# A linear-attention and two-layer MoE kernel: the broadcast of inverse roots to the rows of a head issued per head instead of per pair of heads

## Chip, cores and metric

The kernel runs on one core of one Trainium2 chip. The metric is device time in microseconds (us) of one execution. Three executions of the kernel before took 1691.96, 1692.08 and 1693.05 us; their median, 1692.08 us, is the time before.

## What is computed

The reference is a linear attention over 8 batches, 8 heads, 576 positions and a head size of 64, with a root-mean-square normalization of each position of each head, and then two pairs of dense layers on the 4608 tokens (batch times position) of width 512, each with an inner width of 2048:

```python
kv = einsum('bhsd,bhse->bhde', k, v)
out = einsum('bhsd,bhde->bhse', q, kv)
rms = sqrt(mean(out * out, axis=-1) + 1e-06)
x = (out / rms * g_norm)              # to (4608, 512)
h = x @ w1_in;  x = (s * relu(h)**2 + b) @ w1_out
h = x @ w2_in;  out = (h * sigmoid(1.702 * h)) @ w2_out
```

The part that matters here is `out / rms`: one number, the inverse root, belongs to each of the 8 heads and each token, and must multiply the 64 rows of that head.

## The kernel before

Tokens lie along the free dimension. They are cut into nine blocks j of 512 tokens. A block's attention output is four tiles of 128 rows (two heads of 64 rows each) by 512 tokens, one per pair p. All matmuls of the dense layers are done in a high and a low part (three products in place of one), and most blocks go through a seven-product scheme (`PRODUCTS`) in place of eight plain products.

`events` is a list written by hand: each step has a slot number, the list is sorted by slot, and every engine and queue gets its instructions in that one order. Nearly all transfers are issued from one queue, that of SyncE (SP), in that order. A transfer on SP takes one of eight completion semaphores in turn (DMAHW0 to DMAHW7 in the order listings below), and waits until the transfer eight places before it, which had the same one, has landed.

For the blocks j = 1 to 8, `attend` (line 745) places the attention. The steps that the prediction speaks of, by line:

- `att_product` (L342) and `att_square` (L351) make the output and its squares; `block_mean` (L396) adds the squares of each head on TensorE, so that the result has one row for 16 partitions per head; `block_root` and `block_newton` (L363 to L370) make the inverse roots.
- `y_store` (L411) writes the eight rows of inverse roots, 8 x 512 floats or 16 KB, to a buffer in HBM, `yd[j]`.
- `y_load` (L416) reads them back for each pair p: two rows of 2 KB each, each written to 64 partitions of the tile `yb`, 256 KB in all. It must wait until the store has landed. There are 4 such loads a block, 32 in the program.
- `att_scale` (L421, VectorE) multiplies the attention output by `yb`; `att_split` then splits the result in high and low part (L438, L441) for the first blocks, or stores it (L428) in HBM for the blocks from 3 on.

Behind a block's four `y_load` there stand on SP, by part of the program: loads of raw weights (L133, L138) for the conversion of the first layer's weights, loads of q (L293) and of k and v (L275, L278, L280) for later blocks, stores of converted weights (L190, L203, L243), and in the seven-product part the loads of weights `wl` (L254), each of which feeds two products of TensorE (L565). In the plain part TensorE's steps are `mlp_h` (L479) and `mlp_o` (L522).

Of the kernel before, what the change touches and what calls it, by code (L numbers as in the profile page):

```python
# [14 lines left out]
T = 512  # L15
B, H, S, D = 8, 8, 576, 64
# [47 lines left out]
def kernel(ctx: ExitStack, tc: tile.TileContext, q_h, kv_h, kt, vt, cst,  # L64
# [6 lines left out]
    nc = tc.nc  # L71
# [22 lines left out]
    def new2(dtype, name):  # L94
        return new(mid, [P, T], dtype, name)
# [174 lines left out]
    yd = [dp.tile([H, T], F32, name=f"yd{j}") for j in range(NB)]  # L270
# [142 lines left out]

    def y_load(j, p):
        y = new2(F32, "yb")
        nc.sync.dma_start(out=y, in_=yd[j][2 * p:2 * p + 2].unsqueeze(1).to_broadcast([2, D, T]))  # L416
        att[j, p] = (att[j, p][0], y)

    def att_scale(j, p):
# [325 lines left out]
    def attend(j, slot, gap, late):  # L745
        for g in range(NG):
            at(slot - 4 + g, q_load, j, g)
            at(slot + gap * g, att_product, j, (2 * g, 2 * g + 1))
            for r in range(2):
                at(slot + gap * g + 0.4 + 0.3 * r, att_square, j, 2 * g + r)  # L750
                at(slot + gap * g + 0.4 + 0.3 * r, att_copy, j, 2 * g + r)
        slot += gap + 1.4
        at(slot, block_mean, j)
        at(slot + 0.5, block_root, j)
        at(slot + 1.2, block_newton, j)
        at(slot + 1.8, y_store, j)
        for p in range(NP):
            at(slot + 2.7, y_load, j, p)
            at(slot + late + 1.1 * p, att_scale, j, p)
            at(slot + late + 1.1 * p + 0.3, att_split, j, p)  # L760
# [263 lines left out]
```

## Time and profile before

| | |
|---|---|
| Median of three executions | 1692.08 us |
| Profiled execution, its own time | 1698.42 us |
| Span of the profile | 1696.6 us |
| Mean granted clock of TensorE | 0.956 |
| TensorE matmul busy | 1553.9 us, 92% of the span |
| VectorE, ScalarE busy | 63% and 47% |
| DMA moved | 392.09 MB, mean 231 GB/s |

The span runs from the first to the last instruction; the execution's own time is 1.8 us longer. The profiled execution is 6.3 us longer than the median. Busy shares are averages over the whole span: the first 750 us hold the attention, the conversion of the weights and the plain part, the rest is nearly all matmul. "SPq" is the SP queue issuing a transfer; the time of such a row is that of the issue, not of the transfer.

### The profile page before, as it was taken

To read this page: it belongs to the slowest core of one execution; us is meant where nothing else is said; L and a number is where in the kernel's file an instruction comes from. 1 tells how busy PE (TensorE), PEld (TensorE's weight loads), DVE (VectorE), ACT (ScalarE), POOL (GpSimd) and SP (SyncE) were. 2 spreads that over 40 slices of the span, in tenths; PEclk is the share of its full clock that TensorE was granted. 3 is DMA by queue.
4 is the path that set the end of the run, shared out by engine and by line. 5 is a ranking of instruction groups with operands and counts; after the bars stand their busy time and mean duration, and the time that the engine had idled before them with its cause. 6 is when DMAs were issued, how large, how long until landed. Compare 5 with 4: busy or idle time off the path is not lost.

```text
span 1696.6 us, 20384 instructions
## 1 busy us (share of the span) xinstructions
PE 1553.9 (92%) x7316; PEld 1251.2 (74%) x7316; DVE 1065.3 (63%) x1535; ACT 794.0 (47%) x1162; POOL 1.5 (0%) x12
## 2 busy tenths in 40 slices
PE   7978995969966997879999999999999999999999
PEld 4656764758654875658888888888888888888887
DVE  5966352535654855549467437977896888579522
ACT  5967441425545834558259522542443245135222
POOL 0000000000000000000000000000000000000000
PEclk8999996979987999879999999999999999999999
DMA  9435337496677875698698257678578757837590
GB/s 313 146 108 184 128 139 257 150 315 226 225 256 252 309 231 209 226 327 279 209 387 285 99 217 263 231 273 305 189 266 306 276 198 274 291 106 246 195 328 25
DMA packets 176484, 392.09 MB, mean 231 GB/s; under 512 B 21952, under 2 KB 53696, under 8 KB 176384
## 3 DMA queue, kind: packets, MB, share of 16 engines
q1 hardware_dynamic: 176384, 390.79, 65.9%
q8 instruction: 58, 0.95, 0.2%
q14 instruction: 42, 0.34, 0.1%
HBM read 300.42 MB, written 90.31 MB: 230 GB/s over the span
## 4 chain that ended last, share of the span: by engine, by line
PE 76%; DMA 13%; DVE 6%; SPq 3%; ACT 1%; issue 1%; DVEq 0%; ACTq 0%
PE o L522 22%; PE o L693 18%; PE a L565 8%; PE d L565 8%; PE h L479 6%; PE b L565 4%; PE c L565 4%; PE f L565 4%; DMA wl<-wsd 3%; DMA raw<-in_w_in 1%; DMA wsd<-op 1%; DMA qq<-in_q 1%; DVE cu L157 1%; DMA yb<-yd 1%; DMA raw<-in_w_out 1%; SPq L416 1%
## 5 line engine op out<-in xcount | busy, mean ns | idle before, releaser
L522 PE MATMUL o<-gh,w 128*128 128x512 f32 x1280 | 408.3, 392 | 1.0 <-DVE w L173 0.8
L522 PEld LDWEIGHTS o<-gh,w 128*128 128x128 f32 x1280 | 241.0, 189 | 57.7 <-issue 3.5
L693 PE MATMUL o<-gh,wl 128*128 128x512 f32 x896 | 276.4, 389 | 0.0
L522 PE MATMUL o<-gl,w 128*128 128x512 f32 x640 | 250.2, 391 | 0.3 <-DVE gl L512 0.2
L565 PE MATMUL a<-xh,wl 128*128 128x512 f32 x448 | 160.7, 400 | 45.8 <-DMA wl<-wsd 45.8
L693 PEld LDWEIGHTS o<-gh,wl 128*128 128x128 f32 x896 | 168.2, 188 | 34.9
L479 PE MATMUL h<-xh,w 128*128 128x512 f32 x512 | 173.9, 401 | 17.8 <-ACT w L168 9.9
L565 PE MATMUL d<-xh,wl 128*128 128x512 f32 x448 | 157.9, 393 | 19.9 <-DMA wl<-wsd 16.1
L693 PE MATMUL o<-gl,wl 128*128 128x512 f32 x448 | 174.3, 389 | 0.0
L522 PEld LDWEIGHTS o<-gl,w 128*128 128x128 f32 x640 | 120.7, 189 | 25.8 <-DVE gl L512 1.2
L565 PEld LDWEIGHTS a<-xh,wl 128*128 128x128 f32 x448 | 86.2, 192 | 67.8 <-issue 34.4
L479 PEld LDWEIGHTS h<-xh,w 128*128 128x128 f32 x512 | 97.7, 192 | 47.4 <-ACT w L168 10.3
L581 ACT ACTIVATE c<-a 128x512 f32<-128x512 f32 x56 | 33.4, 597 | 194.9 <-PE a L565 192.0
L565 PEld LDWEIGHTS d<-xh,wl 128*128 128x128 f32 x448 | 84.6, 189 | 40.4 <-issue 16.4
L479 PE MATMUL h<-xl,w 128*128 128x512 f32 x256 | 101.6, 397 | 0.4 <-DVE xl L441 0.4
L693 PEld LDWEIGHTS o<-gl,wl 128*128 128x128 f32 x448 | 84.1, 188 | 17.5
L636 DVE TENSOR_TENSOR gl<-r,gh 128x512 fp32r<-128x512 f32 x96 | 65.2, 687 | 40.2 <-PE o L522 23.2
L565 PE MATMUL a<-xl,wl 128*128 128x512 f32 x224 | 89.1, 398 | 0.0
L584 DVE TENSOR_TENSOR u<-b,c 128x512 f32<-128x512 f32 x56 | 38.6, 690 | 79.4 <-PE b L565 49.7
L565 PE MATMUL d<-xl,wl 128*128 128x512 f32 x224 | 87.7, 391 | 0.0
L667 ACT ACTIVATE gh<-t 128x1024 fp32r<-128x1024 f32 x48 | 51.0, 1062 | 72.5 <-DVE t L658 62.4
L620 ACT ACTIVATE r<-r 128x1024 f32<-128x1024 f32 x84 | 84.5, 1052 | 0.0
(114 smaller groups left out, 2539.6 us busy)
## 6 DMA issues: line engine op xcount, KB each, us to landing
wl<-wsd SPq DMA_DIRECT2D x168, 512.0 KB
wl<-wo2S SPq DMA_DIRECT2D x64, 512.0 KB
wsd<-op SPq DMA_DIRECT2D x96, 256.0 KB
w<-wod SPq DMA_DIRECT2D x48, 512.0 KB
wl<-wo2A SPq DMA_DIRECT2D x48, 512.0 KB
raw<-in_w_in SPq DMA_DIRECT2D x32, 512.0 KB
raw<-in_w_out SPq DMA_DIRECT2D x32, 512.0 KB
wl<-wsd SPq DMA_DIRECT2D x56, 256.0 KB
```

Of the source, the lines that this page charges most:

```text
L157: dve.scalar_tensor_tensor(out=t, in0=raw[:, :, 1], scalar=SIGN_TOP, in1=t, op0=ALU.bitwise_and, op1=ALU.bitwise_or)
L416: nc.sync.dma_start(out=y, in_=yd[j][2 * p:2 * p + 2].unsqueeze(1).to_broadcast([2, D, T]))
L479: pe.matmul(h, lhsT=a, rhs=b, start=(n == 0), stop=(n == 3 * NP - 1))
L522: pe.matmul(acc[m, j][c], lhsT=a, rhs=x, start=(f == 0 and n == 0), stop=(f == NF - 1 and n == 2))
L565: pe.matmul(o, lhsT=a, rhs=b, start=(first and n == 0), stop=(n == 5), skip_group_check=not first)
L581: act.activation(st["c1"], st[0], AF.Copy)
L584: dve.tensor_add(out=st["u2"], in0=st[1], in1=st["c1"])
L620: act.activation(R[q, n], R[q, n], fn)
L636: dve.tensor_sub(out=gl, in0=R[q, i][:, half, :], in1=gh.bitcast(F32))
L667: act.activation(hi, src, AF.Copy)
L693: pe.matmul(so[k, d], lhsT=a, rhs=b, start=(first and n == 0 and i == 0 and e == 0), stop=(n == 3 and i == 1 and e == 2), skip_group_check ...
```

## The change

The load of one pair's two rows, [2 heads, 64 copies, 512], becomes two loads, one per head, [64 copies, 512]. The bytes are the same, 256 KB a pair. There are now 64 loads of 128 KB on SP instead of 32 of 256 KB, at the same places in the order.

```diff
     def y_load(j, p):
         y = new2(F32, "yb")
-        nc.sync.dma_start(out=y, in_=yd[j][2 * p:2 * p + 2].unsqueeze(1).to_broadcast([2, D, T]))
+        for h in range(2):
+            nc.sync.dma_start(out=y[h * D:(h + 1) * D], in_=yd[j][2 * p + h:2 * p + h + 1].to_broadcast([D, T]))
         att[j, p] = (att[j, p][0], y)
```

On the SP queue at block 1, in the plain part, this stands before (`yd` is the buffer of inverse roots, `raw` a tile of raw weights; a name with _49 is a semaphore):

```order
L133 DMA raw<-in_w_in 128x4x256 [waits DMAHW0_49,Activation_49]
L416 DMA yb<-yd_139 128x1x512 [waits DMAHW7_49,DMAHW1_49,PE_49]
L416 DMA yb<-yd_139 128x1x512 [waits DMAHW2_49,PE_49]
L416 DMA yb<-yd_139 128x1x512 [waits DMAHW3_49,Activation_49]
L416 DMA yb<-yd_139 128x1x512 [waits DMAHW4_49]
L138 DMA raw<-in_w_out 128x1024 [waits DMAHW5_49]
L133 DMA raw<-in_w_in 128x4x256 [waits DMAHW6_49]
```

and this now:

```order
L133 DMA raw<-in_w_in 128x4x256 [waits DMAHW0_49,Activation_49]
L417 DMA yb<-yd_139 64x512 [waits DMAHW7_49,DMAHW1_49,PE_49]
L417 DMA yb<-yd_139 64x512 [waits DMAHW2_49]
L417 DMA yb<-yd_139 64x512 [waits DMAHW3_49,PE_49]
L417 DMA yb<-yd_139 64x512 [waits DMAHW4_49]
L417 DMA yb<-yd_139 64x512 [waits DMAHW5_49,Activation_49]
L417 DMA yb<-yd_139 64x512 [waits DMAHW6_49]
L417 DMA yb<-yd_139 64x512
L417 DMA yb<-yd_139 64x512 [waits DMAHW0_49]
L138 DMA raw<-in_w_out 128x1024 [waits DMAHW1_49]
L133 DMA raw<-in_w_in 128x4x256 [waits DMAHW2_49]
```

The eight loads take all eight semaphores, so the raw load behind them waits for the first of them (DMAHW1), where before it waited for a transfer issued ahead of them (DMAHW5).

The same at block 5, in the seven-product part, before (`wsd` holds converted weights, `op` and `wl` are tiles of them, `x0d` holds the scaled attention output `oc`):

```order
L416 DMA yb<-yd_143 128x1x512 [waits DMAHW4_49,PE_49]
L416 DMA yb<-yd_143 128x1x512 [waits DMAHW5_49,PE_49]
L243 DMA wsd_0_104<-op 128x512 [waits DMAHW6_49,Activation_49]
L243 DMA wsd_0_104<-op 128x512 [waits DMAHW7_49]
L254 DMA wl<-wsd_4_100 128x1024 [waits DMAHW0_49]
L254 DMA wl<-wsd_4_100 128x512 [waits DMAHW1_49]
L254 DMA wl<-wsd_5_101 128x1024 [waits DMAHW2_49]
L428 DMA x0d_125<-oc 128x512 [waits DMAHW3_49,DVE_49]
L254 DMA wl<-wsd_5_101 128x1024 [waits DMAHW4_49]
```

and now:

```order
L417 DMA yb<-yd_143 64x512 [waits DMAHW0_49,PE_49]
L417 DMA yb<-yd_143 64x512 [waits DMAHW1_49]
L243 DMA wsd_0_104<-op 128x512 [waits DMAHW2_49,Activation_49]
L243 DMA wsd_0_104<-op 128x512 [waits DMAHW3_49]
L254 DMA wl<-wsd_4_100 128x1024 [waits DMAHW4_49]
L254 DMA wl<-wsd_4_100 128x512 [waits DMAHW5_49]
L254 DMA wl<-wsd_5_101 128x1024 [waits DMAHW6_49]
L429 DMA x0d_125<-oc 128x512 [waits DMAHW7_49,DVE_49]
L254 DMA wl<-wsd_5_101 128x1024 [waits DMAHW0_49]
```

The order of the steps is the same. Each of the eight transfers behind the broadcasts now waits for one of the eight, and the store of the first scaled tile (L428, now L429) still waits for VectorE. The other engines have the same instructions in the same order.

## Rows read from the trace of the kernel before

**Rows 1.** The page: busy tenths of PE, and GB/s moved, in 40 slices.

```profile
PE   7978995969966997879999999999999999999999
...
GB/s 313 146 108 184 128 139 257 150 315 226 225 256 252 309 231 209 226 327 279 209 387 285 99 217 263 231 273 305 189 266 306 276 198 274 291 106 246 195 328 25
```

**Rows 2.** Windows around the eight broadcasts: stretch, length, busy time by engine, clock, DMA share, GB/s.

```profile
95.00:140.00 45.00, 30.25 (x117) 23.00 (x115) 31.00 (x55) 26.12 (x46) 0.00 (x0) 0.85 0.53 164
190.00:225.00 35.00, 29.40 (x129) 22.84 (x128) 13.74 (x22) 13.73 (x21) 0.00 (x0) 0.90 0.48 166
242.00:295.00 53.00, 33.07 (x185) 26.91 (x183) 17.18 (x31) 12.13 (x19) 0.00 (x0) 0.74 0.60 214
318.00:362.00 44.00, 28.93 (x178) 23.86 (x177) 15.90 (x30) 11.13 (x18) 0.00 (x0) 0.81 0.62 212
450.00:492.00 42.00, 25.79 (x126) 19.41 (x125) 17.93 (x32) 16.27 (x25) 0.00 (x0) 0.84 0.58 180
502.00:540.00 38.00, 21.39 (x87) 17.26 (x86) 19.20 (x33) 20.18 (x28) 0.00 (x0) 0.78 0.59 199
650.00:692.00 42.00, 25.95 (x105) 19.99 (x104) 19.38 (x33) 16.71 (x24) 0.00 (x0) 0.80 0.60 200
705.00:742.00 37.00, 21.85 (x83) 17.16 (x82) 18.26 (x32) 15.63 (x20) 0.00 (x0) 0.77 0.55 184
```

**Rows 3.** Timeline of PE, first matmuls behind the stalls of blocks 1, 3 and 6.

```profile
126.78 0.80 PE L479 MATMUL h<-xh,w 128*128 128x512 f32 x1 [9.88 <-ACT w L168]
...
275.30 0.44 PE L311 MATMUL kv<-v_in,k_in 128*64 128x64 f32 x2 [12.27 <-DMA v_in<-in_kv]
...
530.93 0.77 PE L565 MATMUL a<-xh,wl 128*128 128x512 f32 x1 [16.61 <-DMA wl<-wsd]
```

**Rows 4.** Two-us windows inside the broadcast of block 1.

```profile
106.00:108.00 2.00, 2.00 (x10) 1.68 (x9) 1.90 (x5) 0.42 (x1) 0.00 (x0) 1.00 0.13 51
108.00:110.00 2.00, 2.00 (x10) 1.66 (x9) 1.90 (x4) 1.35 (x3) 0.00 (x0) 1.00 0.13 51
```

**Rows 5.** Timeline of the SP queue at block 3 (start, us, issues).

```profile
242.42 0.61 SPq L411 DMA_DIRECT2D yd<-y  x1
244.24 9.33 SPq L416 DMA_DIRECT2D yb<-yd  x4
253.93 5.87 SPq L203 DMA_DIRECT2D wsd<-w  x2
```

**Rows 6.** Single lines' issues on SP: count, ns minimum, median, maximum.

```profile
L416 SPq DMA_DIRECT2D yb<-yd x32: 487/1700/5581, 97.8 to 710.7; - x32
...
L300 SPq DMA_DIRECT2D qq<-in_q x8: 471/533/620, 4.5 to 12.3; - x8
```

**Rows 7.** Other windows, for what the DMA engines reach, and VectorE.

```profile
4.00:5.00 1.00, 1.00 (x6) 1.00 (x6) 0.00 (x0) 0.00 (x0) 0.00 (x0) 1.00 1.07 372
...
690.00:700.00 10.00, 10.00 (x51) 6.41 (x51) 5.09 (x8) 8.17 (x12) 0.00 (x0) 1.00 1.03 388
...
100.00:110.00 10.00, 10.00 (x46) 8.29 (x45) 9.63 (x18) 7.16 (x13) 0.00 (x0) 1.00 0.16 60
```

**Rows 8.** The chain of waits, in order of time, at blocks 6 and 8.

```profile
530.93 2.90 PE a L565 x6
533.83 1.92 PE f L565 x6
...
712.59 1.36 PE c L565 x6
...
733.52 2.92 PE a L565 x6
736.44 2.56 PE b L565 x6
739.00 1.74 PE c L565 x6
```

**Rows 9.** Waits, by line.

```profile
DVE oc L421 <- DMA yb<-yd: 65.3, 23, 5.0
```

## The prediction

> **What bounds the kernel now.** I began with the slices of the page [rows 1]. From slice 20 on (about 850 us) TensorE stands at 9 throughout; nothing this change touches happens there. The holes are all before it, and the GB/s of these slices swing from about 100 to over 300. So I went through the first 760 us in windows of 10 us, and found that the deep holes stand shortly behind the eight broadcasts. Cut to one window per broadcast [rows 2], TensorE is idle there for the length less its busy time: 14.8, 5.6, 19.9, 15.1, 16.2, 16.6, 16.1 and 15.2 us, 119.4 us together.
>
> Next I asked what ends each stall. In the seven-product part it is a load of weights (the 16.61 us at block 6), at block 3 loads of k and v, at block 1 a converted weight whose raw load was late [rows 3]. None of them is the broadcast itself: they stand behind it on SP. So the reader should look at what the broadcast does to the transfers behind it.
>
> While it runs, the DMA engines move 51 GB/s at a share of 0.13 [rows 4]. A share of 0.13 is 2 of 16 engines, and two is the number of rows that a load names outermost. Where other loads run, 372 and 388 GB/s are reached at a share of about 1 [rows 7]. Four loads of 262,144 bytes at 51.2 GB/s take 20.5 us. During that time SP is held up too: the four issues at block 3 take 9.33 us, and two ordinary stores behind them 5.87 us [rows 5]; one broadcast issue takes up to 5.58 us against at most 0.62 us for a load of 64 rows of q [rows 6]. So whatever is issued next has a share on the two engines which lands only when these have emptied.
>
> **What the change does, part by part.**
>
> *The transfer.* The outermost dimension becomes 64 copies in place of 2 heads. The nearest row for such a load is L300, which also fills 64 partitions with rows of 2 KB, and is issued at 4.5 us: the window there shows 372 GB/s and a share of 1.07 [rows 6, 7]. So the 1.05 MB of a block would take 2.8 us at best. At worst, by the row of the present broadcast (51 GB/s), it takes 20.5 us, or more if something new holds it back (a rival, below). I take the fast end because L300 has the same shape on the SBUF side.
>
> *The issues.* Eight per block at L300's median of 0.533 us take 4.3 us, where four now take 9.3 [rows 5, 6]. This is longer than the transfer, so the queue is free again 4.3 us after the broadcast begins, and the DMA engines nearly so. The 32 added issues cost 32 x 0.53 = 17 us of SP in all; they lie within the 4.3 us per block and take the place of a longer stall.
>
> *The semaphores.* All eight are taken by the broadcast, so the eight transfers behind it wait for one broadcast load each. The store of the roots bounds a landing: issued at 242.42, it had landed by 244.24, when the first broadcast was issued, 1.8 us [rows 5]. The first broadcast is 4.3 us old when the transfer behind it comes. I cost this wait at nothing; its cover is those 4.3 us, and a broadcast landing later than that after its issue would hold SP.
>
> *What arrives earlier.* Transfers behind the broadcast land 20.5 - 4.3 = 16.2 us earlier. A stall shrinks by as much, and not below zero. Saved idle time by block [rows 2]: 14.8, 5.6, 16.2 (of 19.9), 15.1, 16.2, 16.2 (of 16.6), 16.1, 15.2, in sum 115.4 us. VectorE's waits for `yb`, 65.3 us [rows 9], go too, but they lie beside the same stalls and are not counted again; the stores of scaled tiles on SP, which wait for VectorE, move with them.
>
> *The clock.* After a stall TensorE restarts at the lower of its levels. At block 8 three groups of six matmuls take 2.92, 2.56 and 1.74 us where 1.36 is usual: 3.1 us lost; at block 6 two groups lose 2.1 [rows 8]. I take 2.6 for each stall that closes, 7 x 2.6 = 18.2 us (block 3 keeps a part of its stall, so none there).
>
> *What is late next: VectorE.* At block 1 VectorE has 31.0 us of work in the window of 45 us [rows 2], and it is full at 9.63 of 10 us when nothing holds it [rows 7]. It cannot do that in less than 32.2 us, so the window gives 12.8 us at most, not 14.8 + 2.6: take off 4.6 us.
>
> *What is late next: the DMA engines.* The bytes of each window stay, and the time shrinks. Window length times GB/s [rows 2], over the shortened length, asks for 308, 355, 326, 394, 360 and 354 GB/s at blocks 3 to 8 (blocks 1 and 2 about 230). The highest window of 10 us shows 388 [rows 7], and mixtures with stores and short rows will not hold that. At 85% of it, 330 GB/s, the windows of blocks 4, 6, 7 and 8 are longer than TensorE needs by 2.0, 3.7, 2.1 and 1.4 us, 9 us in sum. At 388 it is below 1 us, at 300 it is 22 us. I take 330 because these windows mix 512 KB loads with stores and loads of shorter rows.
>
> *Sum.* 115.4 + 18.2 - 4.6 - 9 = 120 us. The profiled execution, 1698.4 us, would become 1578.4. It stands 6.3 us above the median of the runs shown, and the stalls are in every run, so I take the same 120 us from the median: 1692.1 - 120 = **1572 us**. With 1 us in place of 9 for the DMA engines it is 1564, with 22 it is 1585. The most there is to win is all idle time and 21 us of clock (8 x 2.6), 140 us: 1552.
>
> A rule of the Trainium skill speaks against the change. DMA: Bandwidth & Descriptors, section Rules for kernel authors, says of two transfers to the two partition halves not to bother, since they run on the same engines and serialize, and advises one transfer to all 128 partitions. Its premise, that a transfer uses all 16 engines, does not hold here by the share of 0.13. The same section limits a transfer to as many engines as its outermost dimension counts, a leading broadcast dimension included; by that rule, the trace agrees for the 2 heads, and 64 copies may use all 16. No run yet shows a broadcast of 64 copies.
>
> **The rivals.**
>
> *The DMA engines become the bound.* Every stall ends in a burst, and the queue loses the time in which it caught up. If the mixture holds only the 231 GB/s that is the mean of the whole execution, the windows of blocks 3 to 8 exceed what TensorE needs by 12.3, 14.1, 9.5, 13.5, 13.0 and 10.3 us, 73 us in place of my 9, and 1636 us remain. It decides below about 300 GB/s. For it: VectorE, ScalarE and SP wait for each other around transfers, and loads have little lead. Against it: windows with 388 GB/s while TensorE is full.
>
> *One after another.* If each half waits for the one before, a block costs 8 x (1.8 + 0.35) = 17.2 us in place of 20.5 (a landing as the root store's, and 131,072 bytes at 372 GB/s). It saves 8 x 3.3 = 26 us: 1666. Against it: the window at 4 to 5 us reaches 372 GB/s with several loads of 128 and 256 KB in flight. The rule on partition halves, above, is the page that would have this.
>
> *It stays on two engines.* Then nothing moves faster, and the added issues, up to 17 us, are either hidden in a stalled queue or not: 1692 to 1709. Nothing in the rows excludes that a source row repeated 64 times is handled as one; L300's source has 64 different rows.
>
> *Slower: one row in HBM read by all engines.* Today each row of roots is read by one engine, at 25.6 GB/s. Then 16 engines read the same 2 KB. If one row gave no more than those 25.6 GB/s, the eight loads would take 41 us in place of 20.5, the transfers behind wait on all engines instead of two, and 8 x 20.5 = 164 us are added: 1856. It decides where one row gives less than 51 GB/s. Against it: 25.6 GB/s is what an engine gives anyway (388 over 16 is 24), so the row is not what limits it today. No row shows many engines on one address.
>
> **How the numbers follow.** Forecast 0.74 (its own range 1557 to 1592), DMA bound 0.15, one after another 0.03, two engines 0.03, hot row 0.05. The predicted time is the forecast's. From 1552, all idle time and clock gone, to 1625, which takes in most of the DMA rival, some 0.85 is held; I keep it so because the catching up is the least certain term. What counts as a change here is 0.2%, 3.4 us. Faster: 0.74 + 0.15 + 0.03 = 0.92; same: most of two engines, 0.02; slower: hot row and the rest, 0.06.
>
> **What would show it.** Right: windows inside a broadcast with over 300 GB/s at a share near 1; issues of L417 near 0.5 us; the SP queue through the eight in about 4 to 5 us; no stall of TensorE over 5 us behind a broadcast except at block 3; the wait of `att_scale` for `yb` near zero; the mean clock above 0.956; nothing changed behind 850 us but its place in time. The DMA rival shows as stalls of 5 to 14 us with GB/s at 230 to 300 through the whole stretch between. The hot row shows as a share near 1 with some 25 to 50 GB/s. The forecast is wrong if the stalls behind blocks 5 to 8 stay at half their size or more although the broadcast is fast: then the transfers behind it were late for another reason, such as the wait for VectorE or a buffer.

## The result and the profile after

The changed kernel takes 1582.9 us (median of 4 executions, 1580.6 to 1584.3) against 1692.6 us before (4 executions, 1692.0 to 1695.9): a ratio of 0.9347, 95% interval 0.9330 to 0.9364. That is 109.6 us less; 1572 us had been forecast, 120 us less, and the time lies in the range.

The profiled executions allow an account, since every us of the span is either matmul on TensorE or idle there. Before, the span of 1696.6 us held 1553.9 us of matmul, so 142.7 us idle. The page of the changed kernel, its total and its slices of TensorE and of GB/s, against [rows 1]:

```profile
span 1581.9 us, 20440 instructions
...
PE 1538.5 (97%) x7316; PEld 1238.8 (78%) x7316; DVE 1063.5 (67%) x1535; ACT 793.4 (50%) x1162; POOL 1.6 (0%) x12
...
PE   7988998999899999999999999999999999999999
...
GB/s 303 190 121 187 202 160 283 259 266 319 267 333 336 214 316 334 379 187 339 332 297 16 303 223 239 273 300 199 264 287 301 171 271 281 259 139 206 223 311 27
```

Now 1538.5 us are matmul and 43.4 idle: 99.3 us of idle time are gone, and 15.4 us of matmul time, at the same 7316 matmuls. The latter goes with the slow restarts: all of it lies in the first 850 us of the kernel before, and the mean granted clock went from 0.956 to 0.990. The deep holes of the slices are gone.

What the broadcast does to SP can be seen at block 3, the same place as in [rows 5] (timeline of the SP queue: start, us, issues):

```profile
223.25 0.58 SPq L411 DMA_DIRECT2D yd<-y  x1
225.04 4.94 SPq L417 DMA_DIRECT2D yb<-yd  x8
230.03 1.10 SPq L203 DMA_DIRECT2D wsd<-w  x2
```

Eight issues take 4.94 us where four took 9.33, and the two stores behind them 1.10 us where they took 5.87. The line of the broadcast alone (issues with minimum, median and maximum in ns, and the time from issue to landing), SP's eight issues at block 1, and two windows inside the broadcast there, against [rows 4, 6]:

```profile
L417 SPq DMA_DIRECT2D yb<-yd x64: 444/587/1253, 99.3 to 615.5; - x64
...
DMA to landing us min/median/max: 2.8/3.1/6.0
```

```profile
99.33 5.64 SPq L417 DMA_DIRECT2D yb<-yd  x8
```

```profile
102.00:104.00 2.00, 2.00 (x11) 1.65 (x10) 1.97 (x4) 1.46 (x3) 0.00 (x0) 1.00 0.67 204
104.00:106.00 2.00, 2.00 (x10) 1.67 (x9) 1.90 (x5) 1.97 (x4) 0.00 (x0) 1.00 0.66 205
```

The DMA engines move 204 GB/s at a share of 0.67 where they moved 51 at 0.13. They are not full. One load of 131,072 bytes in 0.62 us, the pace of the issues at block 3 (4.94 / 8), is 212 GB/s, and in 0.70 us, the pace at block 1 (5.64 / 8), 186 GB/s. That is about what is moved, so the issues set the pace. VectorE's wait for `yb`, 65.3 us before [rows 9], is 2.6 us (total, times, longest):

```profile
DVE oc L422 <- DMA yb<-yd: 2.6, 2, 2.2
```

What is left of the stalls, in the timeline of TensorE (the bracket is the idle time ahead of the instruction and what ended it), at blocks 1, 3, 4, 5 and 8:

```profile
129.61 0.74 PE L480 MATMUL h<-xh,w 128*128 128x512 f32 x2 [1.97 <-DVE w L173]
...
246.17 0.30 PE L311 MATMUL kv<-v_in,k_in 128*64 128x64 f32 x2 [2.05 <-DMA v_in<-in_kv]
249.06 0.45 PE L311 MATMUL kv<-v_in,k_in 128*64 128x64 f32 x2 [2.59 <-DMA v_in<-in_kv]
251.42 3.24 PE L311 MATMUL kv<-v_in,k_in 128*64 128x64 f32 x58 [1.92 <-DMA v_in<-in_kv]
255.89 0.66 PE L315 MATMUL kv<-tail_v,tail_k 128*64 128x128 f32 x8 [1.23 <-DMA tail_v<-in_vt]
...
306.37 0.30 PE L311 MATMUL kv<-v_in,k_in 128*64 128x64 f32 x2 [2.09 <-DMA v_in<-in_kv]
307.88 2.52 PE L311 MATMUL kv<-v_in,k_in 128*64 128x64 f32 x57 [1.21 <-DMA v_in<-in_kv]
...
416.28 0.47 PE L566 MATMUL a<-xh,wl 128*128 128x512 f32 x1 [1.03 <-DMA wl<-wsd]
422.20 0.79 PE L566 MATMUL d<-xh,wl 128*128 128x512 f32 x1 [2.95 <-DVE r L592]
...
609.92 0.50 PE L566 MATMUL d<-xh,wl 128*128 128x512 f32 x1 [1.03 <-DVE r L592]
```

Block 1 keeps 4.8 us, of which the 1.97 is the largest piece, block 3 7.8 in four pieces, block 4 3.3, block 5 4.0, block 7 0.5 and block 8 about 1.2; blocks 2 and 6 have none left. In the window from 240 to 260 us, where block 3 stalls, the DMA engines are full:

```profile
240.00:250.00 10.00, 4.87 (x24) 3.52 (x22) 0.55 (x1) 4.01 (x7) 0.00 (x0) 0.87 0.97 337
250.00:260.00 10.00, 7.34 (x81) 6.50 (x82) 3.73 (x6) 0.39 (x1) 0.00 (x0) 0.78 0.99 355
```

### The profile page after: what moved, and what is told of

Same layout as the page of the kernel before. It is cut to its first block, busy times and chain, and to the rows that moved or that the text cites. A ratio compares the mean times of both kernels' runs of the same rounds, so it can differ in the third digit from the quotient of the medians.

```text
span 1581.9 us, 20440 instructions
## 1 busy us (share of the span) xinstructions
PE 1538.5 (97%) x7316; PEld 1238.8 (78%) x7316; DVE 1063.5 (67%) x1535; ACT 793.4 (50%) x1162; POOL 1.6 (0%) x12
## 4 chain that ended last, share of the span: by engine, by line
PE 84%; DMA 6%; DVE 5%; ACT 2%; SPq 1%; issue 1%; DVEq 0%; ACTq 0%
PE o L523 25%; PE o L694 19%; PE d L566 9%; PE a L566 9%; PE h L480 7%; PE b L566 4%; PE f L566 4%; PE c L566 4%; DMA v_in<-in_kv 2%; DMA raw<-in_w_in 2%; DVE cu L157 1%; PE o_ps L342 1%; PE kv L311 1%; DVE ca L158 1%; DMA x0d<-oc 1%
## 5 line engine op out<-in xcount | busy, mean ns | idle before, releaser
L673 DVE TENSOR_TENSOR gl<-r,gh 128x1024 fp32r<-128x1024 f32 x64 | 77.1, 1218 | 6.9 <-ACT gh L668 6.9
```

What stands on the lines that cost most here:

```text
L673: dve.tensor_sub(out=lo, in0=src, in1=hi.bitcast(F32))
```

## Experiments

The theory to be tested: a load runs on as many DMA engines as its outermost dimension allows, up to 16; two busy engines hold a share of every transfer that is issued behind the broadcast; TensorE's stalls are these transfers landing late. Its rivals: the size or number of the loads is what helped, or the hold-up of SP's issues, or merely lead that was missing. All runs are against the kernel before on the same chip, which had medians of 1693 to 1695 us there. They were not all on one chip, so where two changed versions are compared, the difference of their medians and that of their ratios to the kernel before can stand some 2 us apart.

The squares of a head are added with a matrix of 16 equal columns per head, so the tile of roots holds each head's row 16 times. Storing more of these rows gives loads with more rows outermost and no other change. This is used in several experiments.

**Four rows outermost, still one load per pair.** (An edit of the kernel before, as all below except in the last experiment, which says what it is made to.)

```diff
-    yd = [dp.tile([H, T], F32, name=f"yd{j}") for j in range(NB)]
+    yd = [dp.tile([2 * H, T], F32, name=f"yd{j}") for j in range(NB)]
...
-        nc.sync.dma_start(out=yd[j], in_=y[0:P:P // H])
+        nc.sync.dma_start(out=yd[j], in_=y[0:P:P // (2 * H)])
...
-        nc.sync.dma_start(out=y, in_=yd[j][2 * p:2 * p + 2].unsqueeze(1).to_broadcast([2, D, T]))
+        nc.sync.dma_start(out=y, in_=yd[j][4 * p:4 * p + 4].unsqueeze(1).to_broadcast([4, 32, T]))
```

> One load per pair as before, but the store writes each head's roots twice, so that a load names 4 rows outermost, each copied to 32 partitions. Theory (the number of engines, set by the outermost count, decides): the broadcast runs on 4 engines at about 102 GB/s and a share of 0.25, a block takes 10.2 us, the transfers behind it land 10.3 us earlier than before. By block 10.3 us of idle time go, but no more than there is: 10.3, 5.6, 10.3, 10.3, 10.3, 10.3, 10.3 and 10.3, some 78 us; less what the changed kernel lost as well (16 us): 1615 to 1640 us. Rival (what helped is that there are two loads of 128 KB in place of one of 256 KB): nothing changes, 1692 us. Rival (any copy spread over more than two engines gives all): 1583 us.

Measured: 1621.0 us, a ratio of 0.9562 (0.9540 to 0.9584), within the theory's band, and neither 1692 nor 1583. A window inside the broadcast, and the SP queue and later restarts of TensorE:

```profile
100.00:102.00 2.00, 2.00 (x11) 1.65 (x10) 1.97 (x4) 1.43 (x4) 0.00 (x0) 1.00 0.29 109
```

```profile
97.51 2.44 SPq L416 DMA_DIRECT2D yb<-yd  x4
100.01 1.84 SPq L138 DMA_DIRECT2D raw<-in_w_out  x1
...
430.55 0.77 PE L565 MATMUL a<-xh,wl 128*128 128x512 f32 x1 [5.77 <-DMA wl<-wsd]
...
614.51 0.76 PE L565 MATMUL d<-xh,wl 128*128 128x512 f32 x1 [5.35 <-DMA wl<-wsd]
```

The share of 0.29 at 109 GB/s is about that of four engines. The four issues take only 2.44 us, less than the eight of the changed kernel, and yet TensorE waits 5.8 us at block 5, 8.8 at block 6 and 5.4 at block 7 for loads of weights behind them.

At block 5 the hold-up of SP and the late landing can be told apart. The product that stalls there needs the first of three loads of weights that stand on SP behind the broadcast. SP's issues of the broadcast and of these loads, first in the kernel before (with the stall), then with four rows, then in the changed kernel:

```profile
451.86 10.18 SPq L416 DMA_DIRECT2D yb<-yd  x4
467.75 1.90 SPq L254 DMA_DIRECT2D wl<-wsd  x3
...
479.78 0.76 PE L565 MATMUL a<-xh,wl 128*128 128x512 f32 x1 [15.08 <-DMA wl<-wsd]
```

```profile
412.00 2.79 SPq L416 DMA_DIRECT2D yb<-yd  x4
417.90 1.87 SPq L254 DMA_DIRECT2D wl<-wsd  x3
```

```profile
402.39 6.34 SPq L417 DMA_DIRECT2D yb<-yd  x8
409.88 1.67 SPq L254 DMA_DIRECT2D wl<-wsd  x3
```

From the start of the broadcast to the issue of the load it is 15.9, 5.9 and 7.5 us, and from there to the stalled product's start 12.0, 12.7 and 6.4. So with four rows the load is issued no later than in the changed kernel and takes 6 us longer from there: the busy engines delay what is issued behind. Of the 14.0 us between the kernel before and the changed one, 8.4 are the earlier issue and 5.6 the time from issue to use, so the hold-up of SP was the larger part at this block. With four rows SP is not free of the broadcast either: its waits for a landing of `yb` are 41 us in all, against 36 before and none in the changed kernel.

**Two loads of 128 KB per pair, each with two rows outermost.**

```diff
-    yd = [dp.tile([H, T], F32, name=f"yd{j}") for j in range(NB)]
+    yd = [dp.tile([2 * H, T], F32, name=f"yd{j}") for j in range(NB)]
...
-        nc.sync.dma_start(out=yd[j], in_=y[0:P:P // H])
+        nc.sync.dma_start(out=yd[j], in_=y[0:P:P // (2 * H)])
...
-        nc.sync.dma_start(out=y, in_=yd[j][2 * p:2 * p + 2].unsqueeze(1).to_broadcast([2, D, T]))
+        for h in range(2):
+            nc.sync.dma_start(out=y[h * D:(h + 1) * D], in_=yd[j][4 * p + 2 * h:4 * p + 2 * h + 2].unsqueeze(1).to_broadcast([2, D // 2, T]))
```

> Two loads of 128 KB per pair, as in the changed kernel, but each names 2 rows outermost (the store writes each head's roots twice, each copy goes to 32 partitions). Theory (number of engines): the loads stay on two engines at 51 GB/s and a share of 0.13, a block still takes 20.5 us, the stalls stay: 1685 to 1705 us. Rival (size and number of the loads): as the changed kernel, about 1583 us.

Measured: 1700.4 us, a ratio of 1.0032 (1.0017 to 1.0046), within the theory's band. A window inside the broadcast, SP at block 3 and the stall of block 6:

```profile
106.00:108.00 2.00, 2.00 (x11) 1.65 (x10) 1.90 (x5) 1.97 (x5) 0.00 (x0) 1.00 0.15 51
```

```profile
249.65 12.46 SPq L417 DMA_DIRECT2D yb<-yd  x8
262.16 3.73 SPq L203 DMA_DIRECT2D wsd<-w  x2
...
536.28 0.77 PE L566 MATMUL a<-xh,wl 128*128 128x512 f32 x1 [18.55 <-DMA wl<-wsd]
```

The same 64 loads of 128 KB as in the changed kernel, on two engines, win nothing and lose 6 us (0.3%): on two engines the split as such is a small cost. The rival falls.

**Sixteen rows outermost, one load per pair.** As the four rows above, with 8 in the place of 2:

```diff
+    yd = [dp.tile([8 * H, T], F32, name=f"yd{j}") for j in range(NB)]
...
+        nc.sync.dma_start(out=yd[j], in_=y[0:P:P // (8 * H)])
...
+        nc.sync.dma_start(out=y, in_=yd[j][16 * p:16 * p + 16].unsqueeze(1).to_broadcast([16, 8, T]))
```

> One load of 256 KB per pair, that names 16 rows outermost, each copied to 8 partitions; the store writes each head's roots 8 times, 128 KB in place of 16. Theory (number of engines): as fast as the changed kernel or a little faster, since four issues of about 0.5 us take 2 us in place of 4.9: the transfers behind come 2 to 3 us earlier, which counts at the blocks that still stall (3, 4 and 5): 1574 to 1583 us. Rival (16 engines on one row of HBM hold each other up in the changed kernel): a broadcast lands clearly earlier here, under 2.5 us, and the time falls below 1574 us. Rival (the split in two loads is needed): near 1692 us.

Measured: 1576.8 us, a ratio of 0.9305 (0.9288 to 0.9323); 6 us below the changed kernel by the medians, 7 by the ratios. The line of the broadcast with its time to landing, and a window:

```profile
L416 SPq DMA_DIRECT2D yb<-yd x32: 528/550/703, 99.2 to 610.4; - x32
DMA to landing us min/median/max: 3.1/4.7/8.9
```

```profile
100.00:102.00 2.00, 2.00 (x11) 1.65 (x10) 1.93 (x4) 1.97 (x4) 0.00 (x0) 1.00 0.95 319
```

With half the issues the broadcast moves 319 GB/s at a share of 0.95. A load of 256 KB lands in 3.1 us at best, one of 128 KB in the changed kernel in 2.8. The sizes differ: 131,072 bytes at 319 GB/s are 0.4 us, and 3.1 less that is 2.7, an estimate. So 16 engines reading one row of 2 KB are not visibly held up by each other, though a few tenths of a us would not show; the landing under 2.5 us and the time below 1574 us of that rival did not come.

**No broadcast.**

```diff
     def y_load(j, p):
-        y = new2(F32, "yb")
-        nc.sync.dma_start(out=y, in_=yd[j][2 * p:2 * p + 2].unsqueeze(1).to_broadcast([2, D, T]))
-        att[j, p] = (att[j, p][0], y)
+        att[j, p] = (att[j, p][0], None)
...
-        dve.scalar_tensor_tensor(out=o, in0=o, scalar=g_col, in1=y, op0=ALU.mult, op1=ALU.mult)
-        drop(y)
+        dve.scalar_tensor_tensor(out=o, in0=o, scalar=g_col, in1=o, op0=ALU.mult, op1=ALU.mult)
```

> Leaves out the broadcast: the roots are stored but not loaded back, and the scaling multiplies the attention output by itself in place of the roots. It shows what is left to win from the broadcast. Theory (in the changed kernel the broadcast costs only its 4.9 us of SP a block, which counts at the blocks that still stall): 1568 to 1582 us, with the stall at block 3 shorter but not gone. Rival (the DMA engines are the bound in the stretches behind the broadcasts, so that its 8.4 MB count in full): 8.4 MB at some 340 GB/s are 25 us, 1555 to 1562 us.

Measured: 1573.6 us, a ratio of 0.9281 (0.9265 to 0.9297), within the theory's band. Without any broadcast the kernel is only 9.3 us faster than the changed one by the medians (11 by the ratios), and the changed one had won 109.6: the broadcast costs some 10 us now, where it cost about 120. The stall at block 3 is still there without it, 0.94, 2.61, 1.71 and 1.50 us:

```profile
244.47 0.30 PE L311 MATMUL kv<-v_in,k_in 128*64 128x64 f32 x2 [0.94 <-DMA v_in<-in_kv]
247.37 0.30 PE L311 MATMUL kv<-v_in,k_in 128*64 128x64 f32 x2 [2.61 <-DMA v_in<-in_kv]
```

So most of what is left of that stall was another one, hidden under the first.

**Eight rows outermost.** As above, with 4 in the place of 2.

> One load per pair that names 8 rows outermost, each copied to 16 partitions; the store writes each head's roots 4 times. Theory (number of engines): 8 engines, some 205 GB/s, 5.1 us a block. Transfers behind the broadcast land 5.1 - 2.5 us later than with 16 engines and one load per pair, which had 1576.8 us; of that only what exceeds the slack counts: 1579 to 1592 us, near the changed kernel. With the four points 2, 4, 8 and 16 engines the time should fall by less at each step. Rival (the step from two engines matters, not the count): 1621 us, as with four.

Measured: 1588.2 us, a ratio of 0.9378 (0.9357 to 0.9399), within the theory's band. A window inside the broadcast of block 3:

```profile
229.00:231.00 2.00, 2.00 (x11) 1.65 (x10) 0.94 (x2) 0.71 (x2) 0.00 (x0) 1.00 0.45 158
```

With one load per pair and 2, 4, 8 and 16 rows outermost the windows show shares of 0.13, 0.29, 0.45 and 0.95, and the kernel takes 1692.6, 1621.0, 1588.2 and 1576.8 us: each doubling wins less than the one before, as stalls close.

**The broadcast on ScalarE's queue.**

```diff
-        nc.sync.dma_start(out=y, in_=yd[j][2 * p:2 * p + 2].unsqueeze(1).to_broadcast([2, D, T]))
+        nc.scalar.dma_start(out=y, in_=yd[j][2 * p:2 * p + 2].unsqueeze(1).to_broadcast([2, D, T]))
```

> The kernel before, with the broadcast (two rows outermost, one load per pair) issued from ScalarE's queue instead of SP's. Theory (the transfers behind the broadcast wait because they stand in the same queue of the two engines): on another queue they take turns with it and land earlier, so TensorE's stalls behind loads shrink to a few us; ScalarE is held up at the issues instead, some 9 us a block, part of which shows as waits of TensorE for ScalarE: 1600 to 1660 us. Rival (the two engines' capacity itself is what is missing): stalls behind loads stay over 10 us and ScalarE's hold-up comes on top: 1692 us or more.

Measured: 1712.1 us, a ratio of 1.011 (1.009 to 1.013). The number is the rival's, the picture only in part. ScalarE's queue and its next instruction, then TensorE at blocks 1 and 3:

```profile
102.12 17.26 ACTq L416 DMA_DIRECT2D yb<-yd  x4
119.42 0.66 ACT L144 ACTIVATE ca<-raw 128x512 uint32<-128x512 uint32 x1 [16.68 <-issue]
...
123.72 0.79 PE L522 MATMUL o<-gh,w 128*128 128x512 f32 x1 [12.17 <-ACT gh L503]
...
283.36 0.44 PE L311 MATMUL kv<-v_in,k_in 128*64 128x64 f32 x2 [13.34 <-DMA v_in<-in_kv]
```

Four issues hold ScalarE for 17.3 us at block 1, twice what I had put down, while the DMA engines, with the loads from SP beside the broadcast, move 367 and 384 GB/s (104 to 108 us); TensorE's stall there is behind ScalarE. Behind loads of k and v there remain 13.3, 3.6, 3.9 and 1.6 us at block 3, which is the rival's picture, and 6.6, 6.6 and 3.5 at block 4. Behind a single load of weights nothing over 2.5 us is left; the stalls of that part now end with VectorE or ScalarE, up to 10 us. SP itself stands for 132 us in waits that the profile puts down to a landing of `yb`, 36 before. My expectation missed; how much of the stalls a queue of its own would take away, without the hold-up of ScalarE, stays open.

**Earlier loads of k and v.** The edit is made to the version with 16 rows outermost, to the changed kernel, and to the kernel before:

```diff
-            at(slot - 3.3 + 0.5 * p, kv_load, b, p)
-        at(slot - 1.3, tail_load, b)
+            at(slot - (5.3 if b > 3 else 3.3) + 0.5 * p, kv_load, b, p)
+        at(slot - (3.3 if b > 3 else 1.3), tail_load, b)
```

> The version with 16 rows outermost (1576.8 us), and for the batches from 4 on the loads of k, v and their tails stand 2 slots (some 5 us) earlier in the order. What is left of stalls at blocks 3 and 4 is 6.6, 2.9 and 3.0 us before the kv products, with the DMA engines at 310 to 355 GB/s. If these loads are late because they are issued late, most of it goes: 1565 to 1572 us. If the DMA engines are the bound there, other transfers come later by as much and the time stays within 3 us: 1574 to 1580 us.

> The changed kernel, with the loads of k, v and their tails for the batches from 4 on 2 slots earlier. The same edit took 15 us from the version with 16 rows outermost. If what the changed kernel still loses at blocks 3 and 4 (7.8 and 3.3 us of idle time, and the slow restart) comes from these loads being issued late, it wins about as much: 1566 to 1572 us. If 16 rows outermost were needed for it, under 5 us: 1578 or more.

> The kernel before with the same earlier loads of k, v and tails. If the stalls of 19.9 and 15.1 us at blocks 3 and 4 come from the broadcast that stands ahead, 5 us of lead take at most 5 us from each: 1680 to 1690 us. If lead alone was what was missing, they go, and some 40 us with the slow restarts: 1650 us.

Measured: 1561.8 us with 16 rows (ratio 0.9230, 0.9215 to 0.9245), 1568.5 us with the changed kernel (0.9268, 0.9246 to 0.9290), 1687.3 us with the kernel before (0.9957, 0.9942 to 0.9972). So the loads were issued late; by the medians 15, 14 and 8 us are won by 2 slots of lead, by the ratios 13, 13 and 7. With 16 rows the time is 3 us under the range that I had expected; the other two lie in theirs. At block 3 the changed kernel with this edit stalls 1.01 us ahead of the kv products, the kernel before still 7.29, 2.70, 0.85 and 3.07 (first line the changed kernel, second the kernel before):

```profile
244.66 1.93 PE L311 MATMUL kv<-v_in,k_in 128*64 128x64 f32 x58 [1.01 <-DMA v_in<-in_kv]
```

```profile
271.50 0.45 PE L311 MATMUL kv<-v_in,k_in 128*64 128x64 f32 x2 [7.29 <-DMA v_in<-in_kv]
```

Two slots of lead do not repair the kernel before, where the spread of the broadcast has to come first; more lead, or lead for the loads of weights, was not tried. The version with 16 rows outermost and earlier loads is the fastest found, 1561.8 us.

## Why the prediction was right, and where it was off

*The transfer and the issues.* The broadcast left the two engines; the experiments with 2 to 16 rows outermost show that it is the outermost count, and the one with two loads on two engines that it is not the split. Here the Trainium skill has both rules in one section (DMA: Bandwidth & Descriptors, Rules for kernel authors): the outermost dimension bounds the number of engines, and two transfers to the partition halves are not worth it. On the first the trace agrees, with shares of 0.13, 0.29 and 0.95 for 2, 4 and 16 rows. The second holds between equals: one load with 16 rows beats two loads with 64 copies by 6 us, and two loads on two engines lose 6 us to one. It was the first rule that decided this change.

The issues were put at 4.3 us a block and measured 4.9 to 6.3 (0.62 us each in a row of eight, where L300's median gave 0.53). The transfer is then not the 372 GB/s of the forecast but 204, set by the issues. The step on the issues had this in it (1.05 MB in 4.3 us are 244 GB/s); the sign "over 300 GB/s at a share near 1" went against that step and did not come. The 372 GB/s were also not L300's. Its first issue only starts at 4.50 us, half way through that window, as SP's timeline of the kernel before shows, and what moved there had been issued ahead of it:

```profile
4.50 1.26 SPq L300 DMA_DIRECT2D qq<-in_q  x2
```

So no row of the kernel before bore on whether 64 copies spread; that they do is shown only now, by the share of 0.67. The wait for the semaphores, put at nothing, is nothing: the changed kernel's trace has no wait of SP for a landing of `yb`.

*What arrives earlier, and what is late next.* Idle time left behind the broadcast, by block, as the prediction's terms leave it and as measured, in us:

| Block | 1 | 2 | 3 | 4 | 5 | 6 | 7 | 8 | sum |
|---|---|---|---|---|---|---|---|---|---|
| Forecast | 4.6 | 0 | 3.7 | 2.0 | 0 | 4.1 | 2.1 | 1.4 | 17.9 |
| Measured | 4.8 | 0 | 7.8 | 3.3 | 4.0 | 0 | 0.5 | 1.2 | 21.6 |

The term for VectorE at block 1 came out to a few tenths, and nearly all of its stalls end with VectorE, as forecast. The sum is near only because larger errors offset each other, and that is luck.

At block 3 the step that failed is the one on shrinking stalls: it took the stall as the broadcast's alone, less 16.2 us, and the loads of k and v were late by themselves, as the run without a broadcast shows. At block 5 I counted on nothing, and a wait for VectorE of 2.95 us stands there, where the kernel before had 1.13. In the chain of waits it goes back to a store of a scaled tile (7.05 us). With eight rows outermost it is 2.96, with sixteen 1.04, and without the broadcast it is gone; what makes that store late stays open.

The 9 us put down for the DMA engines at blocks 4, 6, 7 and 8 are the mis-sized term in the other direction: no run shows them. What is left at block 4 is gone with earlier loads of k and v, the pieces at 7 and 8 are waits for VectorE (the 1.03 at block 8 was there before, too), and at block 6 more than the 330 GB/s of the forecast are held with TensorE full:

```profile
450.00:470.00 20.00, 20.00 (x90) 16.57 (x89) 15.21 (x27) 19.97 (x29) 0.00 (x0) 1.00 0.98 355
```

*The clock.* 18.2 us were forecast, 15.4 measured: block 5, whose stall did not close, still restarts slowly (2.92 us for six matmuls where 1.36 is usual). Block 3 does too, as the forecast had it.

*From the profile to the median.* Idle time and clock together are 114.7 us between the two profiled executions, against 120 forecast. By the medians it is 109.6. The step that took the profiled execution's gain unchanged for the median was off by 5 us: the profiled execution of before was 6 us above its median, that of the changed kernel 1 us. So the account of the profile holds a surplus that the median does not, and it should have been left out of the gain; what the surplus was, one profiled execution of each does not show.

*The rivals.* The DMA engines as the bound: they are full where block 3 stalls, for a few us, but loads issued 2 slots earlier take most of that stall away. One after another: no, a landing takes 2.8 us at least and eight loads are issued in 4.9. Two engines: no. The hot row: no sign of it in the landing times; a few tenths of a us would not show.

## What to carry to other kernels

Look at the DMA share while a transfer runs, not only at its place in the chain: a share of 0.13 that lasts for 20 us names a transfer on two engines, and the waits that it causes carry the names of the transfers behind it. For a broadcast, write the access so that at least 16 rows or copies stand outermost; if the source exists several times on chip, storing it often enough to load with 16 rows (here each head's row 8 times) was 6 us better than splitting the load. When a stall goes, run once with the cause left out altogether: it tells what is still to win (here some 10 us) and which stall was hidden beneath (here loads issued too late, worth 13 to 15 us).

## What the runs showed of the hardware that had not been expected

Whether an issue holds up its queue goes, in these runs, with how much is outstanding per engine: four loads that put 32 rows of 2 KB on each of their four engines were issued in 2.44 us at block 1 (2.4 to 3.9 over the blocks), four with 64 rows on each of two engines in 9.33, and eight with 32 rows on each of two engines in 12.46. That is 128 rows per engine in the first case and 256 in the others; where between them a limit lies was not tried. When the held-up queue was ScalarE's, the same four issues took 17.3 us at block 1, and its arithmetic stood for 16.7 us.

Sixteen engines reading the same 2 KB of HBM showed no cost that these runs could measure: 2.8 us at best from issue to landing for 128 KB from one row (median 3.1), 3.1 for 256 KB from sixteen (median 4.7).
